# Splitting float32 operands on another engine, and finishing attention blocks in smaller steps

## The chip, the cores and the metric

The kernel runs on one core of a Trainium2 chip. The metric is the device time of one execution in microseconds. The engines are TensorE (PE in the profile; PEld is its loading of weights), VectorE (DVE), ScalarE (ACT), GpSimd (POOL) and SyncE (SP), which issues most of the DMAs.

## What is computed

For x of 2048 x 512 in float32:

```python
qkv = x @ wqkv                                   # 32 heads of 16
scores = einsum("hqd,hkd->hqk", q, k) * 16**-0.5
scores = where((q - k >= 0) & (q - k < 256), scores, -1e9)
a = (softmax(scores) @ v) @ wo
b = (silu(x @ w_gate) * (x @ w_up)) @ w_down     # width 1792
g = sigmoid((x * gate_w).sum(-1))
out = g * a + (1 - g) * b
```

## The kernel before, in words

**Two halves.** Each float32 operand of a large product is split into a high half (rounded to the type that TensorE takes at full speed) and a low half, `src - high` (`split`, lines 68 to 73). A product is three matmuls: high by high, high by low, low by high. ScalarE casts the high half; the low half is one subtraction of two operands in SBUF, on GpSimd or VectorE as the caller says.

**Start (lines 401 to 512).** The first weights of Q and K (groups 0 and 1) come in two pieces each; `split_wq` splits a piece. x comes in four chunks of 512 columns, each of four k blocks; `split_x(c)` splits a chunk, its low halves on VectorE. V's weights (four k blocks, `wvh`, `wvl`) are split in the loop of lines 484 and 485: high on ScalarE, low on GpSimd for even k and on VectorE for odd k. TensorE then computes the first projections (`proj`), the first four blocks of V (`vproj`, each 12 matmuls that go through k in order: high by high, high by low, low by high), and further projections. `put_v` is ScalarE's copy of a V block out of PSUM. After this come the row maxima of group 0.

**The main loop (lines 697 to 726)** has 129 turns `t`. Heads are in eight groups of four; a turn handles one block of 128 queries or keys of one group, and has four *steps*, one a head. Four turns make a *quad*, numbered here from 0 (`d` in the code), with parts 0 to 3; step (p, h) is step h of part p. In each step the program order is:

- `stage1` of the next group: a score matmul (line 302) into one of two PSUM banks `ps1`, and VectorE's masked row maximum (line 304, followed by a short instruction that reads out the accumulator). The score matmul of a step can start only when the maximum two steps before is done. Only quads 0 to 27 have this stage.
- `stage2` of this group: a score matmul the other way round (line 344), ScalarE's exp (line 346), and in every second step GpSimd's `affine_select` (lines 348, 351), which zeroes what the window leaves out.
- six matmuls of a projection or of the FFN (line 252).
- what was put into `AT` for this step: splits, FFN products, loads.
- one step of `finish`, where the list of line 714 says so.

**Finishing a block of values.** In step (0,1) of each quad from 1 on, `av` multiplies the probabilities of the quad before by V (line 368), into two PSUM tiles. `finish` (lines 375 to 399) then runs in steps, as a Python generator that is advanced by `run(FIN, 1)`: ScalarE copies one tile (line 383), VectorE adds the other (385, and 387 in some quads), transposes (389), takes the reciprocal of the softmax sums and multiplies by it (393, 394; 128 x 256 elements), and transposes back (397); GpSimd issues the DMA to DRAM (398). Each `yield` ends a step. Before the change the steps are: copy in (0,1), addition in (0,2), transposition in (1,1), reciprocal with multiplication in (1,3), transposition and DMA in (2,1).

**What else stands in `AT`.** `halve_next` splits the next FFN or projection weights: ScalarE casts, GpSimd subtracts (`wl`, line 73, 128 x 512). Lines 546 to 559 put it at step 1 of part 0, or at step 0 of part 2 or of part 3. `group_half` splits the projections of a later group (`xlo`, line 73, also GpSimd) in steps (0,0) to (1,1) of some quads. VectorE's products of the FFN (lines 571 and 583) stand in (3,0), (3,1), (3,3) and (0,0), a sum (585) in (1,0). In quads 26 to 31 the token gate's products (638) stand in (1,2) and (2,2), and from quad 28 on the splits of w_down (`early`, lines 641 to 663, with casts at line 654) in part 0.

Each engine takes its instructions in program order; the order above is written out by hand.

Of the kernel before, what the change touches and what calls it, by code (L numbers as in the profile page):

```python
# [12 lines left out]
ALU = mybir.AluOpType  # L13
# [3 lines left out]
P = 128  # L17
S, D, H, DH, W, F = 2048, 512, 32, 16, 256, 1792
NK = D // P
NB = S // P  # L20
CH = 512
# [15 lines left out]
def gated_mix(ctx, tc, xT, xn, wqk, wv, wo, wgu, wd, gw, outT):  # L37
# [4 lines left out]
    nc = tc.nc  # L42
# [25 lines left out]
    def split(hi, lo, src, hi_eng, lo_eng):  # L68
        if hi_eng is nc.scalar:
            nc.scalar.copy(hi, src)  # L70
        else:
            hi_eng.tensor_copy(hi, src)
        lo_eng.tensor_tensor(out=lo, in0=src, in1=hi.bitcast(F32), op=ALU.subtract)

    def fetch(src, raw=None):

        raw = ring.tile([P, D], F32, name="raw", bufs=1) if raw is None else raw
        nc.sync.dma_start(raw, src)
        return raw

    def by_k(t):
        return t.rearrange("p (k n) -> p k n", k=NK)
# [11 lines left out]
    def run(gen, n=None):  # L94

        while n is None or n > 0:
            if next(gen, run) is run:
                break
            n = n and n - 1
# [73 lines left out]
    def prefetch():  # L173
        if WKEYS:
            PEND.append(weights(WKEYS[0], lo_eng=nc.vector if WKEYS.pop(0) == ('f', NF - 1, 0) else nc.gpsimd))
# [25 lines left out]
    with ExitStack() as A:  # L201
# [14 lines left out]
        def kept():  # L216
            return sm.tile([P, CH], F32, name="ev", bufs=EV)
# [10 lines left out]
        def whole(pool, name, todo, done):  # L228

            ps = pool.tile([P, CH], F32, name=name)  # L230
            for n, (w, x) in enumerate(todo):
                nc.tensor.matmul(ps, w, x, start=n == 0, stop=n == len(todo) - 1)  # L232
                if n < len(todo) - 1:
                    yield
            done(ps)
            yield
# [91 lines left out]
        def load_v(n):  # L328

            VG[n] = sm.tile([P, 4, VW], F32, name="vg", bufs=4)  # L330
            nc.sync.dma_start(VG[n], vd[n // 4, :, n % 4 * 4:n % 4 * 4 + 4])
# [43 lines left out]
        def finish(g, c):  # L375


            first, second = AV[g, c]
            if not AB:
                AB.extend(osb.tile([P, CH], F32, name=f"o{n}") for n in range(2))  # L380
            both, ot = AB[::-1] if c % 2 else AB
            lo = 0 if c else 64
            nc.scalar.copy(both[:, lo:], second[:, lo:])
            yield
            nc.vector.tensor_tensor(out=both[:, lo:], in0=first[:, lo:], in1=both[:, lo:], op=ALU.add)  # L385
            if lo:
                nc.vector.tensor_copy(both[:, :lo], first[:, :lo])
            yield
            nc.vector.transpose(ot, both)
            yield  # L390
            v = ot.rearrange("p (s e) -> p s e", e=32)
            rc = osb.tile([P, CH // 32], F32, name="rc")
            nc.vector.reciprocal(rc, v[:, :, DH])
            nc.vector.tensor_tensor(out=v[:, :, :DH], in0=v[:, :, :DH],
                                    in1=rc[:, :, None].to_broadcast([P, CH // 32, DH]), op=ALU.mult)
            yield
            nc.vector.transpose(both, ot)
            nc.gpsimd.dma_start(od[g, :, c * CH:(c + 1) * CH], both)
            yield
# [3 lines left out]
        wvh = vpool.tile([P, NK, D], F32R, name="wvh")  # L403
        wvl = vpool.tile([P, NK, D], F32R, name="wvl")
# [8 lines left out]
        def split_wq(g, n, lo_eng):  # L413
            if n == 0:
                WT["p", g] = [ring.tile([P, D], F32R, name=w) for w in ("wh", "wl")]
            hi, lo = (w[:, QUARTERS[n]] for w in WT["p", g])
            split(hi, lo, WQ[g][:, QUARTERS[n]], nc.scalar, lo_eng)
            if n == 1:
                WT["p", g] = [by_k(w) for w in WT["p", g]]
# [3 lines left out]
        def fill_rows(tiles, value, hf, eng):  # L423
            for t in tiles:
                eng.memset(halves_of(t)[hf].bitcast(F32), value)
# [3 lines left out]
        def fill_v(t):  # L429
            nc.gpsimd.memset(t, 0.0)  # L430
            for i in range(2):
                nc.gpsimd.memset(t[:, :, i, :68].rearrange("p g (j e) -> p g j e", e=17)[:, :, :, DH], 1.0)
# [3 lines left out]
        def v_products(b):  # L436
            c, o = divmod(b * P, CH)
            return [(xt[c][:, k, o:o + P], wt[:, k]) for k in range(NK)
                    for xt, wt in ((xhi, wvh), (xhi, wvl), (xlo, wvh))]

        def put_v(b, ps):
            t = vs[b // 2 % 2]
            nc.scalar.copy(t[:, :, b % 2, :68].rearrange("p g (j e) -> p g j e", e=17)[:, :, :, :DH],
                           ps.rearrange("p (g j e) -> p g j e", j=4, e=DH))
            if b % 2:
                nc.gpsimd.dma_start(vd[:, :, b - 1:b + 1].rearrange("g p b e -> p g (b e)"),
                                    t.rearrange("p g b e -> p g (b e)"))

        def vproj(b):
            return whole(pp, "pb", v_products(b), lambda ps: put_v(b, ps))  # L450
# [11 lines left out]
        def split_x(c, ks=range(NK)):  # L462
            for k in ks:
                split(xhi[c][:, k], xlo[c][:, k], xraw[2 * c + k // 2][k % 2], nc.scalar, nc.vector)

        for c in range(NCH):
# [7 lines left out]
            if c == 0:  # L474
                wvraw = [fetch(wv[:, k], kept()) for k in range(NK)]
        split_wq(0, 0, nc.gpsimd)
        split_x(0, range(1))
        split_wq(1, 0, nc.vector)
        split_wq(0, 1, nc.gpsimd)
        fill_rows(KT[0], 1.0, 0, nc.gpsimd)  # L480
        split_x(0, range(1, 2))
        split_wq(1, 1, nc.vector)
        split_x(0, range(2, NK))
        for k in range(NK):
            split(wvh[:, k], wvl[:, k], wvraw[k], nc.scalar, nc.vector if k % 2 else nc.gpsimd)
        prefetch()
        both = [proj(g, 0, pp, "pa") for g in range(2)]
        for k in range(NK):
            for gen in both:
                run(gen, 3)  # L490
        split_x(1)
        fill_v(vs[1])
        fill_rows(QT[0], 0.0, 1, nc.gpsimd)
        fill_rows(KT[0], 1.0, 1, nc.gpsimd)
        for b in range(2):
            run(vproj(b))
        split_x(2)
        for b in range(2, 4):
            run(vproj(b))
# [43 lines left out]
        def later(t, hd, *fs):  # L543
            AT.setdefault((t, hd), []).extend(fs)
# [65 lines left out]
        def unit(t):  # L610

            def both(n, name):
                key, hf = TURNS[t // 2 + n]
                done = (group_half(t, key[1], hf) if key[0] == "p" else (gate_half, up_half)[key[2]](t, key[1], hf))
                two = []

                def turn(m):
                    if not two:
                        two.extend(lanes(pp, name, [products(key, 2 * hf + m) for m in range(2)], done))
                    yield from two[m]  # L620
                return turn(0), turn(1)
            (a0, a1), (b0, b1) = (both(n, name) for n, name in enumerate(("pa", "pb")))
            return [a0, b0, a1, b1]
# [55 lines left out]
        for b in range(NB):  # L679
            t, hd = blocks[b]  # L680
            later(t, hd, lambda b=b: gate_block(b))
            if b > 1:
                t, hd = blocks[b - 2]
# [13 lines left out]
        FIN = iter(())  # L697
        for t in range(G * NB + 1):
            g, i = divmod(t, NB)
            d, part = divmod(t, NSLOT)  # L700
            if part == 0:
                turns = unit(t) if t < G * NB else [iter(())] * NSLOT
            s1 = stage1(g + 1, i) if t < g7 else iter(())
            s2 = stage2(g, i) if t < G * NB else iter(())
            for hd in range(4):
                run(s1, 1)
                if t < g7:
                    run(s2, 1)
                elif hd % 2 == 0:
                    run(s2, 2)  # L710
                run(turns[part], 3)
                for f in AT.pop((t, hd), ()):
                    f()
                if (part, hd) in ((0, 2), (1, 1), (1, 3), (2, 1)):
                    run(FIN, 1)
                if hd == 1 and part == 0:
                    if t:
                        ag, c = divmod(d - 1, NCH)
                        av(ag, c)
                        FIN = finish(ag, c)  # L720
                        run(FIN, 1)
            if i in (7, 15) and g + 1 < G:
                later(t + 1, 2, lambda g=g, i=i: put_max(g + 1, i // 8))
            if t >= 10 and t % 4 == 2 and t + 6 < G * NB:
                load_v((t + 6) // 4)
# [6 lines left out]
    with ExitStack() as B:  # L732
# [7 lines left out]
        def column():  # L740
            return hp.tile([P, CH], F32, name="sg", bufs=4)
# [300 lines left out]
        for n, e in enumerate(ITEMS[:end]):  # L1042
# [13 lines left out]
            p, k, pr = e  # L1056
# [6 lines left out]
        two, t, part, rest = bank(4, 1), *(column() for _ in range(3))  # L1063
# [46 lines left out]
```

## Time and profile before

| | us |
|---|---|
| median of 3 runs | 803.44 (803.0 to 803.46) |
| the profiled execution, its time | 803.47 |
| its span, first to last instruction | 801.8 |
| TensorE busy | 795.2 (99%) |
| VectorE busy | 627.3 (78%) |
| ScalarE busy | 432.4 (54%) |
| GpSimd busy | 346.2 (43%) |

The times of the profile are measured from the start of the span. An engine's busy time is the union of its instructions. Ends of matmuls are modelled, so their starts are the better measure. "Idle before" in brackets is how long the engine stood idle before an instruction, with what ended the wait.

### The profile page before, as it was taken

Reading aid. Unit: us, or ns where it says so; the run is one execution under the profiler, and the core shown is the slowest. Engines: PE = TensorE matmul, PEld = TensorE weight load, DVE = VectorE, ACT = ScalarE, POOL = GpSimd, SP = SyncE. Lnnn points to the kernel's source line nnn. Section 1 sums busy time; section 2 is a strip of 40 time slices with the busy share of each in tenths; the row PEclk is TensorE's granted clock in tenths of the full one; section 3 lists DMA queues with packets and bytes.
Section 4 is the critical chain, followed back from the end, with each engine's and each line's share of the span. In section 5 each row is a group of like instructions: output and inputs, shape, how many; then the busy total and the mean of one; then the engine's idle time right before and its main releaser. Section 6 shows DMA issues by size and latency. Waiting matters only on the chain.

```text
span 801.8 us, 21443 instructions
## 1 busy us (share of the span) xinstructions
PE 795.2 (99%) x8247; PEld 697.1 (87%) x8247; DVE 627.3 (78%) x1686; ACT 432.4 (54%) x883; POOL 346.2 (43%) x647
## 2 busy tenths in 40 slices
PE   8999999999999999999999999999999999999998
PEld 7888999989889989889998988888988888888886
DVE  6397687878887787878777878888675478899896
ACT  6412656666566566555666656555643235554642
POOL 7821546564546556544656454546740111000212
PEclk9999999999999999999999999999999999999999
DMA  8675414434252453351444516435627898718435
GB/s 298 171 200 164 141 57 135 119 114 137 71 164 78 117 167 94 113 163 54 134 119 130 152 46 200 134 99 181 195 100 240 283 342 300 290 56 275 93 54 104
DMA packets 62107, 121.88 MB, mean 152 GB/s; under 512 B 10868, under 2 KB 19828, under 8 KB 61748
## 3 DMA queue, kind: packets, MB, share of 16 engines
q1 hardware_dynamic: 54900, 99.27, 40.1%
q0 software_dynamic: 7104, 21.24, 9.0%
q8 instruction: 65, 1.06, 0.6%
q14 instruction: 38, 0.31, 0.1%
HBM read 55.97 MB, written 39.34 MB: 119 GB/s over the span
## 4 chain that ended last, share of the span: by engine, by line
PE 96%; DVE 2%; DMA 1%; SPq 0%; POOL 0%; issue 0%; ACT 0%
PE pa L252 24%; PE pb L252 24%; PE ps L302 7%; PE ps L344 5%; PE ps L368 5%; PE ps L89 4%; PE ps L90 4%; PE ps L88 4%; PE pb L368 4%; PE pb L232 2%; PE pb L89 2%; PE pa L89 2%; PE pa L90 2%; PE pb L90 2%; PE pa L88 2%; PE pb L88 2%
## 5 line engine op out<-in xcount | busy, mean ns | idle before, releaser
L304 DVE CUSTOM_DVE_ANT_0 ps<-ps,mask 128x384 f32<-128x384 f32 (+2 forms) x512 | 268.4, 540 | 99.4 <-PE ps L344 52.3
L346 ACT ACTIVATE pt<-ps 128x384 f32<-128x384 f32 (+2 forms) x512 | 238.0, 474 | 127.8 <-PE ps L344 68.0
L348 POOL TENSOR_SCALAR_AFFINE_SELECT pt<-pt 128x256 f32<-128x256 f32 x256 | 110.2, 431 | 198.6 <-ACT pt L346 196.8
L344 PE MATMUL ps<-q,k 64*128 64x384 f32 (+2 forms) x512 | 162.3, 334 | 0.0
L302 PE MATMUL ps<-k,q 63*128 63x384 f32 (+2 forms) x512 | 159.8, 332 | 0.5 <-DVE mx L304 0.5
L252 PE MATMUL pb<-xhi,wh 64*128 64x512 f32 x512 | 116.9, 395 | 0.0
L252 PE MATMUL pb<-xlo,wh 64*128 64x512 f32 x512 | 115.6, 391 | 0.0
L252 PE MATMUL pb<-xhi,wl 64*128 64x512 f32 x512 | 115.6, 391 | 0.0
L252 PE MATMUL pa<-xhi,wh 64*128 64x512 f32 x512 | 115.3, 393 | 0.0
L252 PE MATMUL pa<-xlo,wh 64*128 64x512 f32 x512 | 114.2, 391 | 0.0
L252 PE MATMUL pa<-xhi,wl 64*128 64x512 f32 x512 | 114.2, 391 | 0.0
L302 PEld LDWEIGHTS ps<-k,q 63*128 63x128 f32 x512 | 88.7, 185 | 14.1 <-DVE mx L304 3.7
L351 POOL TENSOR_SCALAR_AFFINE_SELECT pt<-pt 128x256 f32<-128x256 f32 x224 | 98.6, 440 | 0.0
L344 PEld LDWEIGHTS ps<-q,k 64*128 64x128 f32 x512 | 91.1, 184 | 4.9 <-ACT pt L346 0.2
L304 DVE DVE_READ_ACCUMULATOR2_ANT mx<- 128x1 f32 x512 | 71.3, 139 | 0.0
L368 PE MATMUL ps<-pt,vg 64*32 64x320 f32 (+4 forms) x1408 | 70.6, 344 | 0.0
L368 PE MATMUL pb<-pt,vg 64*32 64x256 f32 (+3 forms) x1360 | 69.9, 349 | 0.0
L252 PEld LDWEIGHTS pb<-xhi,wh 64*128 64x128 f32 x512 | 62.8, 185 | 4.1 <-DVE o L385 0.3
L252 PEld LDWEIGHTS pb<-xhi,wl 64*128 64x128 f32 x512 | 62.4, 184 | 3.5
L252 PEld LDWEIGHTS pa<-xhi,wl 64*128 64x128 f32 x512 | 61.1, 185 | 3.9
L252 PEld LDWEIGHTS pb<-xlo,wh 64*128 64x128 f32 x512 | 62.5, 185 | 0.2
L252 PEld LDWEIGHTS pa<-xhi,wh 64*128 64x128 f32 x512 | 60.5, 186 | 1.8
(305 smaller groups left out, 1604.5 us busy)
## 6 DMA issues: line engine op xcount, KB each, us to landing
kept_h<-ev SPq DMA_DIRECT2D x52, 256.0 KB
od<-o POOLq DMA_DIRECT2D x32, 256.0 KB, 3.7
raw<-wgu SPq DMA_DIRECT2D x28, 256.0 KB
q<-xhi SPq DMA_DIRECT2D x56, 128.0 KB
k<-xhi SPq DMA_DIRECT2D x56, 128.0 KB
outT<-sg POOLq DMA_DIRECT2D x28, 256.0 KB, 4.4
vd<-vs POOLq DMA_DIRECT2D x8, 672.0 KB, 4.8
vg<-vd SPq DMA_DIRECT2D x32, 168.0 KB
```

The source lines that it names most:

```text
L88: nc.tensor.matmul(ps, lh, rh, start=start and i == 0, stop=False, skip_group_check=skip)
L89: nc.tensor.matmul(ps, lh, rl, start=False, stop=False, skip_group_check=skip)
L90: nc.tensor.matmul(ps, ll, rh, start=False, stop=stop and i == n - 1, skip_group_check=skip)
L232: nc.tensor.matmul(ps, w, x, start=n == 0, stop=n == len(todo) - 1)
L252: mm = nc.tensor.matmul(ps[me], w[r], x[r], start=not second and i == 0, stop=bool(second) and i == n - 1)
L302: nc.tensor.matmul(ps[:, :n], QT[g % 2][pr][r, q0:q0 + P], KT[g % 2][pr][r, k0:k0 + n], start=True, stop=True)
L304: mx = nc.vector.tensor_tensor_reduce(out=ps[:, :n], in0=ps[:, :n], in1=mask[:, 3 * P - n:], scale=1.0, scalar=NEG, op0=ALU.add, op1=ALU.m ...
L344: nc.tensor.matmul(ps[:, :n], KT[g % 2][pr][r, k0:k0 + P], QT[g % 2][pr][r, k0:k0 + n], start=True, stop=True)
L346: BEHIND.append(nc.scalar.activation(pt[:, j, :n], ps[:, :n], AF.Exp, scale=SCALE))
L348: nc.gpsimd.affine_select(out=pt[:, :, :P], in_=pt[:, :, :P], pattern=[[0, 2], [1, P]], compare_op=ALU.is_ge, fill=0.0, base=0, channel_mu ...
L351: nc.gpsimd.affine_select(out=pt[:, :, 2 * P:], in_=pt[:, :, 2 * P:], pattern=[[0, 2], [-1, P]], compare_op=ALU.is_ge, fill=0.0, base=-1, ...
L368: nc.tensor.matmul(AV[g, c][h][32 * j:32 * j + 32, q0 - c * CH:q1 - c * CH], VG[4 * g + kb // 4][o, kb % 4, 17 * j:17 * j + 32], PT[g, kb, ...
```

## The change

Three edits. First, the low half of the second piece of group 0's weights, and the low halves of V's weights for even k, go from GpSimd to VectorE; the splits of the second x chunk are issued after V's first and second block, two k blocks each. Second, in `finish` the reciprocal is a step of its own, and the multiplication becomes two instructions of 128 x 128 elements, a step each. Third, the list of steps in which `finish` is advanced becomes (0,2), (1,1), (1,3), (2,0), (2,1), (2,2), and the advance comes ahead of `AT` in its step. So the reciprocal stands in (1,3), the halves of the multiplication in (2,0) and (2,1), the transposition with the DMA in (2,2).

```diff
             nc.vector.reciprocal(rc, v[:, :, DH])
-            nc.vector.tensor_tensor(out=v[:, :, :DH], in0=v[:, :, :DH],
-                                    in1=rc[:, :, None].to_broadcast([P, CH // 32, DH]), op=ALU.mult)
             yield
+            for s in (slice(0, CH // 64), slice(CH // 64, CH // 32)):
+                nc.vector.tensor_tensor(out=v[:, s, :DH], in0=v[:, s, :DH],
+                                        in1=rc[:, s, None].to_broadcast([P, CH // 64, DH]), op=ALU.mult)
+                yield
             nc.vector.transpose(both, ot)
...
-        split_wq(0, 1, nc.gpsimd)
+        split_wq(0, 1, nc.vector)
...
-            split(wvh[:, k], wvl[:, k], wvraw[k], nc.scalar, nc.vector if k % 2 else nc.gpsimd)
+            split(wvh[:, k], wvl[:, k], wvraw[k], nc.scalar, nc.vector)
...
-        split_x(1)
         fill_v(vs[1])
...
         for b in range(2):
             run(vproj(b))
+            split_x(1, range(2 * b, 2 * b + 2))
         split_x(2)
...
+                if (part, hd) in ((0, 2), (1, 1), (1, 3), (2, 0), (2, 1), (2, 2)):
+                    run(FIN, 1)
                 for f in AT.pop((t, hd), ()):
                     f()
-                if (part, hd) in ((0, 2), (1, 1), (1, 3), (2, 1)):
-                    run(FIN, 1)
```

## Rows read from the trace of the kernel before

**Rows 1.** The page, busy time and share of the span of each engine.
```profile
PE 795.2 (99%) x8247; PEld 697.1 (87%) x8247; DVE 627.3 (78%) x1686; ACT 432.4 (54%) x883; POOL 346.2 (43%) x647
```

**Rows 2.** Waits of the weight loads: who <- whom: us in total, times, longest.
```profile
PEld ps L302 <- DVE mx L304: 3.7, 11, 0.7
...
PEld pb L232 <- POOL wvl L73: 1.3, 2, 0.9
```

**Rows 3.** Timelines by engine (start, us, engine, line, [idle before]): quad 7; last, quad 15.
```profile
201.07 1.27 POOL L73 TENSOR_TENSOR xlo<-ev,xhi 128x512 fp32r<-128x512 f32 x1
...
201.48 1.15 DVE L394 TENSOR_TENSOR o<-o,rc 128x256 f32<-128x256 f32 x1
202.55 0.55 DVE L304 CUSTOM_DVE_ANT_0 ps<-ps,mask 128x384 f32<-128x384 f32 x1
...
201.71 0.18 PEld L302 LDWEIGHTS ps<-k,q 63*128 63x128 f32 x1
203.22 0.18 PEld L302 LDWEIGHTS ps<-k,q 63*128 63x128 f32 x1 [0.67 <-DVE mx L304]
...
332.38 1.16 DVE L394 TENSOR_TENSOR o<-o,rc 128x256 f32<-128x256 f32 x1
```

**Rows 4.** Line 394: count, ns least/median/most, first and last start.
```profile
L394 DVE TENSOR_TENSOR o<-o,rc x32: 424/474/1155, 103.3 to 602.0; 128x256 f32<-128x256 f32 x32
```

**Rows 5.** Timelines by engine, steps (2,0) to (3,1) of quad 5.
```profile
169.56 1.29 POOL L73 TENSOR_TENSOR wl<-raw,wh 128x512 fp32r<-128x512 f32 x1 [0.38 <-ACT wh L70]
...
169.34 0.57 DVE L304 CUSTOM_DVE_ANT_0 ps<-ps,mask 128x384 f32<-128x384 f32 x1
...
169.83 0.70 DVE L397 STREAM_TRANSPOSE o<-o 128x512 f32<-128x512 f32 x1
...
170.47 0.18 PEld L302 LDWEIGHTS ps<-k,q 63*128 63x128 f32 x1
171.32 0.18 PEld L302 LDWEIGHTS ps<-k,q 63*128 63x128 f32 x1
172.21 0.18 PEld L302 LDWEIGHTS ps<-k,q 63*128 63x128 f32 x1
```

**Rows 6.** Timeline of the start of the kernel.
```profile
5.26 0.28 DVE L73 TENSOR_TENSOR wl<-ev,wh 128x128 fp32r<-128x128 f32 x1
...
6.82 1.01 POOL L73 TENSOR_TENSOR wl<-raw,wh 128x384 fp32r<-128x384 f32 x1 [2.03 <-ACT wh L70]
...
10.09 0.69 DVE L73 TENSOR_TENSOR xlo<-q,xhi 128x512 fp32r<-128x512 f32 x1 [0.64 <-ACT xhi L70]
...
11.02 2.57 ACT L70 CAST wvh<-ev 128x512 fp32r<-128x512 f32 x4 [0.96 <-DMA ev<-wv]
...
11.71 3.00 POOL L73 TENSOR_TENSOR wvl<-ev,wvh 128x512 fp32r<-128x512 f32 x2 [2.11 <-ACT wvh L70]
...
12.01 0.39 PE L232 MATMUL pa<-xhi,wl 128*128 128x512 f32 x1
...
12.23 0.39 PE L232 MATMUL pb<-wvh,xhi 128*128 128x512 f32 x1
...
13.05 0.50 PE L232 MATMUL pb<-wvl,xhi 128*128 128x512 f32 x1 [0.43 <-POOL wvl L73]
```

**Rows 7.** Tile wl alone, busy by stretch, first and last of six (step (2,1)).
```profile
121.00:122.40 1.40, 0.88 (x4) 0.26 (x2) 0.00 (x0) 1.29 (x1) 1.00 0.02 6
...
431.20:432.70 1.50, 0.80 (x4) 0.25 (x4) 0.00 (x0) 1.29 (x1) 1.00 0.00 0
```

The columns are the length, then PE, PEld, DVE and POOL with their counts, the clock, the DMA share and GB/s. The other four stretches begin at 169.5, 251.9, 300.4 and 382.7.

**Rows 8.** Timeline of VectorE, step (2,2) of quad 26.
```profile
515.13 0.68 DVE L638 SCALAR_TENSOR_TENSOR xhi<-xlo,xhi 128x512 f32<-128x512 f32 x1
```

**Rows 9.** Timelines of VectorE and ScalarE, step (0,2) of quad 28.
```profile
539.17 1.85 DVE L654 CAST q<-ev 128x512 fp32r<-128x512 f32 x2
...
541.27 0.65 DVE L385 TENSOR_TENSOR o<-pb,o 128x512 f32<-128x512 f32 x1
...
540.00 0.59 ACT L383 COPY o<-ps 128x512 f32<-128x512 f32 x1 [1.10 <-PE pb L368]
```

## The prediction, made before the changed kernel was run

> **What bounds the kernel now.** I read the page first. TensorE is busy for 99% of the span [rows 1]. So the time changes only where TensorE starts to wait or stops waiting, and a microsecond saved on VectorE or GpSimd is worth nothing by itself. Next I read the list of waits for the engine that loads weights [rows 2]: there the reader sees the two kinds of wait that the change can touch, the score matmul of line 302 waiting for the row maxima of line 304, and the first V matmuls waiting for low halves that GpSimd makes. Last I read the timeline around those places. Sums are made against the profiled execution: 803.47 us, of which 801.8 is its span and 1.67 lies around it; it stands 0.03 over the median of the runs.
>
> **First mechanism: a port that one engine holds.** In quad 7 the multiplication of line 394 starts at 201.48, while GpSimd's subtraction runs from 201.07 to 202.34. It ends at 202.63, so 0.29 after GpSimd [rows 3], and it takes 1.15 where the 32 have a median of 0.47 and a least of 0.42 [rows 4]. It does not run slower, it stands still. The reciprocal just before it was not held (it was over by 201.48, with GpSimd at work since 201.07), nor is a transposition beside such a subtraction (0.70, [rows 5]). The Trainium skill (SBUF — State Buffer, Who interferes with whom) has the rule: a VectorE instruction with two SBUF inputs and a GpSimd instruction that reads SBUF exclude each other, and the one that starts first keeps the port to its end. The trace agrees (1.15 against 0.42); were the bandwidth shared instead, a block would stay within the slack of the two score banks and the term of the six quads below would be near 0, which is the second case's time. This rule speaks for one half of the change and against the other.
>
> **Start: low halves by VectorE.** The second V matmul waits until 13.05 for a low half that GpSimd begins at 11.71; the matmul before it started at 12.23, and these follow each other by 0.22 (12.01 to 12.23), so it came 0.6 late. Of two such waits, 1.3 together, the list puts 0.9 on this one and so 0.4 on a second [rows 2]; the load of weights runs ahead of its matmul, so of the two I count 0.6 and 0.3. ScalarE's four high halves take 2.57 from 11.02, so the first is there at 11.66; VectorE, with nothing of GpSimd beside it, needs 0.69 for such a subtraction (the 512-wide one at 10.09), so the low half is there at 12.4 and the matmul can go at 12.45. The next come every 0.69, as fast as three matmuls of 0.22 use them up. Gain: 0.6 + 0.3 = **0.9**. The first weights' low half (GpSimd, 6.82 to 7.83, [rows 6]) becomes earlier by about 0.4 on VectorE, but that only makes TensorE wait longer for V: 0. Bounds of the stage: 0.5 (the later low halves come late by a little each) to 1.0. Moving the second x chunk's splits behind V's first two blocks costs nothing: their first user is the projection behind four V blocks, 48 matmuls or 10.6 us later, and VectorE has eight subtractions of 0.69, 5.5 us, to do in that time; without this cover a late chunk would cost up to those 5.5. GpSimd's memory fills start earlier and have no reader that waits.
>
> **The finish in smaller steps, ordinary quads.** A full multiplication of 0.42 becomes two of 0.28 (VectorE's two-input instruction of 128 elements at the start took that, [rows 6]); since an instruction starts some 0.07 before the last one ends, VectorE has about 0.1 more work a quad. The score steps last about 0.87 (the weights of line 302 at 170.47, 171.32 and 172.21 are 0.85 and 0.89 apart, [rows 5]), one maximum holds VectorE for 0.5 (169.34 to 169.83), so 0.37 is free in each step: a half of 0.21 net fits, a transposition of 0.63 net is made good by the free step behind it. Cost 0 with that cover; without it 0.1 in each of the 27 quads that have both, 2.7, is the bound. Waits fall on nobody new: the reciprocal's reader now comes one step later. The output DMA on GpSimd's queue goes out one step later, and GpSimd's selects of steps (2,3) and (3,1) queue behind it; their reader is the value sum of the next quad, so 0.
>
> **Two quads gain.** In quad 7 the weights of line 302 are loaded at 201.71 and then at 203.22, 1.51 apart instead of 0.87 [rows 3]: 0.64 lost. Quad 15 has the same pattern (1.16 at 332.38, [rows 3]). With the reciprocal alone in step (1,3), the maximum of (2,0) no longer stands behind the blocked multiplication; the first half then starts near 202.0, is held until 202.34 and ends by 202.48, some 0.1 after the maximum of (2,1) could start, and the two banks hide that. Gain 2 x 0.6 = **1.2**. In the other quads GpSimd's work lengthens the multiplication by less: its median is 0.05 over its least [rows 4], 1.3 for 25 quads; taking that out of a step in which a bank is waited for is worth 0 to 1.3, and I take **0.4**, near the small end, because the waits of line 302 are 3.7 in all, of which 1.3 is already counted [rows 2].
>
> **Six quads lose.** Here the steps were moved past work of GpSimd. Weights' low halves that are due at step (2,0) run on GpSimd in quads 2, 5, 10, 13, 18 and 21, 1.29 in the first and the last [rows 7]. Until now only a transposition ran beside them, and it is not blocked (0.70, [rows 5]). Now the second half stands in its place. In quad 5: GpSimd holds the port from 169.56 to 170.85; the second half comes at 169.83, 0.27 too late, and ends 0.14 after GpSimd (the tail of 0.29, less the 0.14 that 128 elements save). So the maximum of (2,2) starts at 170.92 instead of 170.46. The transposition, now in step (2,2), starts 0.48 later (169.34 to 169.83 shows that step), takes 0.63 net, and the maximum of (2,3) starts at 172.03. Its bank is free 0.62 + 0.05 later (202.55 to 203.22, [rows 3]), at 172.70. The score matmul of step (3,1) wanted it at 172.21: 0.49 lost, of which 0.27 already at (3,0). The other quads, by the same arithmetic, give up to 0.65, as steps alternate in length. I take 0.55: 6 x 0.55 = **3.3** lost (2.9 to 3.9). The lead of GpSimd rests on ScalarE's cast, which follows TensorE and not VectorE, so the change does not move it.
>
> **Two more quads lose a little.** In quads 26 and 27 the token gate's product of line 638, 0.68, already stands in step (2,2) [rows 8], and now the transposition comes into the same step; VectorE is without a gap there, so the second multiplication instruction's 0.1 is paid in each: **0.2** (0.1 to 0.7).
>
> **Order inside a step.** The finish step now comes ahead of what is due in that step. In quad 28 that matters: two casts of 1.85 (blocked by GpSimd) stand in front of the addition of line 385, which frees a bank and starts only at 541.27, 0.68 after ScalarE's copy was there at 540.59 [rows 9]. Now it goes first: gain **0.2** (0 to 0.45).
>
> Sum: -0.9 - 1.2 - 0.4 + 3.3 + 0.2 - 0.2 = +0.8; 803.47 + 0.8 gives 804.3.
>
> **Rivals.** *The six blocks don't happen or are absorbed.* Either the second half comes before GpSimd's subtraction, or the score banks hide the wait. For it: the margin is 0.27 of 1.29. Against it: the same order of start led to the full block in quad 7. The sum without 3.3 is -2.5: 801.0.
> *The blocks cost their whole length.* Place: the same six, steps (2,1) to (3,1). The half (1.16 from 169.83) and the transposition behind it delay the maxima with no slack left, because the two products of line 571 at (3,0) and (3,1) keep VectorE from catching up. Price 1.0 each, 6.0 instead of 3.3: 807.0. From 0.68 a block on, the whole is slower by over 0.2%. For it: both banks are already at their limit in quad 7. Against it: in quad 7 a block of 0.86 cost 0.64.
>
> **How the numbers follow.** 0.2% (1.6 us) is about what a measurement of this kernel can tell from no change: under 801.8, or over 805.0. My case has 0.70; its own range is 803.0 to 805.6, by the bounds above, and it gives 0.48 to no change and 0.22 to slower. The first rival has 0.20 (0.17 faster, 0.03 the same), the second 0.10, all slower. Together: faster 0.17, same 0.51, slower 0.32. The range 800.8 to 805.8 takes in my case and the first rival, and leaves out the second.
>
> **What would show it.** Right: the second V matmul starts by about 12.5; 64 multiplications of about 0.28, of which six last over 1.0, all in step (2,1) of the quads named; the weights of line 302 wait more than the 3.7 of now, with the waits at (3,0) and (3,1) of those six; quads 7 and 15 lose their 0.67. Wrong: no multiplication above 0.6 (then the first rival), or six waits of 1.0 (the second). If the V matmuls still wait beyond 12.5, the start term is wrong; if new waits of line 302 turn up in the other quads, the cover was not there.

## The result and the profile after

The changed kernel takes 806.29 us (median of 11 executions, 804.37 to 808.55) against 803.55 for the kernel before on the same chips (802.54 to 804.38): 1.0033 of it, with an interval of 1.0026 to 1.0041. It is slower, and outside the forecast range.

There are two losses. The profiled execution took 804.64, 1.17 over that of before. It is one of four executions whose mean granted clock is 0.999 or 1.0 (804.37 to 805.29); the other seven have 0.995 to 0.998 and take 806.01 to 808.55. What the four show is told first; the rest is a matter of the clock (experiment 9).

The page again shows a busy TensorE, and VectorE and GpSimd have traded work:

```profile
PE 794.2 (99%) x8247; PEld 686.8 (86%) x8247; DVE 630.9 (79%) x1721; ACT 432.7 (54%) x883; POOL 335.4 (42%) x644
```

To see where the time went, I measure each quad from its first weight load of line 344 to that of the next.

| place | before | after | difference |
|---|---|---|---|
| start, up to quad 0 | 79.70 | 78.78 | -0.92 |
| quads 7, 15 | 16.90 each | 16.40 each | -1.00 |
| quad 23 | 16.74 | 16.40 | -0.34 |
| quads 6, 14, 22 | 16.60, 16.62, 16.62 | 16.43 each | -0.55 |
| quads 2, 5, 10, 13, 21 | 81.61 in all | 83.30 | +1.69 |
| quad 18 | 16.63 | 16.54 | -0.09 |
| quads 26, 27 | 33.53 | 33.41 | -0.12 |
| quad 28 | 15.47 | 17.66 | **+2.19** |
| quad 29 | 14.80 | 14.93 | +0.13 |
| the rest, differences up to 0.05 a quad, and the tail | | | +0.18 |

The start went as forecast. In the timeline of the changed kernel the second V matmul (wvl) follows the first after 0.23, where it came 0.82 after it, at 13.05, before [rows 6]:

```profile
10.75 2.64 DVE L73 TENSOR_TENSOR wvl<-ev,wvh 128x512 fp32r<-128x512 f32 x4 [0.53 <-ACT wvh L70]
...
12.39 0.39 PE L232 MATMUL pb<-wvh,xhi 128*128 128x512 f32 x1
12.62 0.39 PE L232 MATMUL pb<-wvl,xhi 128*128 128x512 f32 x1
```

In quad 7 (timeline of the changed kernel) the weights of line 302 are loaded 0.86 and 0.81 apart, where one gap was 1.51 [rows 3]. The half of the multiplication is still lengthened, but only to 0.50:

```profile
201.63 0.50 DVE L396 TENSOR_TENSOR o<-o,rc 128x128 f32<-128x128 f32 x1
...
201.37 0.18 PEld L302 LDWEIGHTS ps<-k,q 63*128 63x128 f32 x1
...
202.23 0.18 PEld L302 LDWEIGHTS ps<-k,q 63*128 63x128 f32 x1
...
203.04 0.18 PEld L302 LDWEIGHTS ps<-k,q 63*128 63x128 f32 x1
```

The held halves came too. Line 396 with its least, median and longest duration in ns, and rows of quad 5 in the changed kernel, from the second half in step (2,1) to the load of step (3,2):

```profile
L396 DVE TENSOR_TENSOR o<-o,rc x64: 282/289/1262, 102.7 to 603.5; 128x128 f32<-128x128 f32 x64
```

```profile
168.99 1.30 POOL L73 TENSOR_TENSOR wl<-raw,wh 128x512 fp32r<-128x512 f32 x1 [0.56 <-ACT wh L70]
...
169.25 1.19 DVE L396 TENSOR_TENSOR o<-o,rc 128x128 f32<-128x128 f32 x1
170.36 0.55 DVE L304 CUSTOM_DVE_ANT_0 ps<-ps,mask 128x384 f32<-128x384 f32 x1
...
169.90 0.19 PEld L302 LDWEIGHTS ps<-k,q 63*128 63x128 f32 x1
...
171.02 0.18 PEld L302 LDWEIGHTS ps<-k,q 63*128 63x128 f32 x1 [0.29 <-DVE mx L304]
...
172.10 0.18 PEld L302 LDWEIGHTS ps<-k,q 63*128 63x128 f32 x1 [0.36 <-DVE mx L304]
...
172.84 0.18 PEld L302 LDWEIGHTS ps<-k,q 63*128 63x128 f32 x1
```

The half comes 0.26 behind GpSimd's subtraction and ends 0.15 after it, and two loads of line 302 wait, 0.65 together. The next load follows after only 0.74, so part of that is made good: quad 5 is 0.33 longer, not 0.65. In quad 18 the order of the two starts is the other way round, and nothing is held:

```profile
381.94 0.29 DVE L396 TENSOR_TENSOR o<-o,rc 128x128 f32<-128x128 f32 x1
...
382.05 1.34 POOL L73 TENSOR_TENSOR wl<-raw,wh 128x512 fp32r<-128x512 f32 x1 [0.93 <-ACT wh L70]
```

**Quad 28** is the loss that the forecast doesn't have. `put_max` (lines 311 to 321), which is due in step (0,2) of this quad by line 723, turns the row maxima (lines 315, 316), stores them to DRAM (`md`, line 318) and reads them back into the q tiles (line 320), both on SyncE's queue. Behind these two in the queue stand the loads of weights, of xn and of w_down, and then two writes of FFN products (`kept_h`, line 588 before, 590 after). Timelines of VectorE, SyncE's queue (SPq) and ScalarE around it, before:

```profile
535.57 0.27 PEld L344 LDWEIGHTS ps<-q,k 64*128 64x128 f32 x2
...
541.13 0.21 DVE L316 STREAM_TRANSPOSE mtt<-mt 128x32 f32<-128x32 f32 x1
...
541.38 0.58 SPq L318 DMA_DIRECT2D md<-mtt  x1
543.37 0.99 SPq L320 DMA_DIRECT2D q<-md  x2
...
545.80 0.90 SPq L588 DMA_DIRECT2D kept_h<-ev  x2
...
549.87 0.60 ACT L568 ACTIVATE ev<-pa 128x512 f32<-128x512 f32 x1 [0.16 <-DMA kept_h<-ev]
```

and after:

```profile
534.25 0.27 PEld L344 LDWEIGHTS ps<-q,k 64*128 64x128 f32 x2
...
539.30 0.69 DVE L385 TENSOR_TENSOR o<-pb,o 128x512 f32<-128x512 f32 x1 [0.34 <-ACT o L383]
539.91 0.96 DVE L656 CAST q<-ev 128x512 fp32r<-128x512 f32 x2
...
541.20 0.21 DVE L316 STREAM_TRANSPOSE mtt<-mt 128x32 f32<-128x32 f32 x1
...
549.25 0.69 DVE L640 SCALAR_TENSOR_TENSOR xhi<-xlo,xhi 128x512 f32<-128x512 f32 x1 [2.79 <-DMA xlo<-xn]
...
541.44 0.58 SPq L318 DMA_DIRECT2D md<-mtt  x1
544.03 0.99 SPq L320 DMA_DIRECT2D q<-md  x2
...
546.48 0.90 SPq L590 DMA_DIRECT2D kept_h<-ev  x2
...
550.88 0.60 ACT L570 ACTIVATE ev<-pa 128x512 f32<-128x512 f32 x1 [2.87 <-DMA kept_h<-ev]
...
551.91 0.83 PE L344 MATMUL ps<-q,k 64*128 64x384 f32 x2 [2.03 <-ACT pt L346]
```

Read it against the start of the quad. The addition of line 385 now heads the step and waits for ScalarE's copy, which ends at 5.02 in both kernels. (The wait shows as 0.34 here because VectorE's sums before it are held beside GpSimd in this profile; where they are not, in the second profile of the same kernel under experiment 9, it is 1.37, and the addition starts at the same 5.05.) The casts, which began 3.60 after the start (539.17 in [rows 9], less 535.57), begin at 5.66, and `put_max` is behind them. The store goes out at 7.19 instead of 5.81, the read back at 9.78 instead of 7.80, the writes at 12.23 instead of 10.23. ScalarE's tanh (line 570) takes the buffer that such a write empties. It already waited 0.16 for it before; now it waits 2.87, the exps queue behind it, and TensorE stands still for 2.03.

### The profile page after: what moved, and what is told of

It is laid out like the page before. It is cut to its first block, busy times and chain, and to the rows that moved or that the text cites. A ratio compares the mean times of both kernels' runs of the same rounds, so it can differ in the third digit from the quotient of the medians.

```text
span 802.9 us, 21471 instructions
## 1 busy us (share of the span) xinstructions
PE 794.2 (99%) x8247; PEld 686.8 (86%) x8247; DVE 630.9 (79%) x1721; ACT 432.7 (54%) x883; POOL 335.4 (42%) x644
## 4 chain that ended last, share of the span: by engine, by line
PE 96%; DVE 1%; DMA 1%; ACT 0%; SPq 0%; issue 0%
PE pa L252 24%; PE pb L252 24%; PE ps L302 7%; PE ps L368 5%; PE ps L344 5%; PE ps L90 4%; PE ps L89 4%; PE ps L88 4%; PE pb L368 4%; PE pb L232 2%; PE pa L232 2%; PE pa L90 2%; PE pb L90 2%; PE pb L88 2%; PE pa L89 2%; PE pb L89 2%
## 5 line engine op out<-in xcount | busy, mean ns | idle before, releaser
L348 POOL TENSOR_SCALAR_AFFINE_SELECT pt<-pt 128x256 f32<-128x256 f32 x256 | 106.9, 418 | 192.7 <-ACT pt L346 192.0
L252 PE MATMUL pb<-xhi,wh 64*128 64x512 f32 x512 | 111.3, 395 | 0.0
L252 PE MATMUL pa<-xlo,wh 64*128 64x512 f32 x512 | 110.4, 391 | 0.0
L252 PE MATMUL pa<-xhi,wl 64*128 64x512 f32 x512 | 110.1, 391 | 0.0
L252 PE MATMUL pb<-xlo,wh 64*128 64x512 f32 x512 | 109.7, 391 | 0.0
L252 PE MATMUL pb<-xhi,wl 64*128 64x512 f32 x512 | 109.7, 392 | 0.0
L351 POOL TENSOR_SCALAR_AFFINE_SELECT pt<-pt 128x256 f32<-128x256 f32 x224 | 95.5, 427 | 0.0
L252 PEld LDWEIGHTS pb<-xhi,wl 64*128 64x128 f32 x512 | 56.8, 185 | 5.4
L252 PEld LDWEIGHTS pb<-xhi,wh 64*128 64x128 f32 x512 | 56.8, 186 | 4.9
L252 PEld LDWEIGHTS pa<-xhi,wh 64*128 64x128 f32 x512 | 56.7, 186 | 3.1
L252 PEld LDWEIGHTS pa<-xlo,wh 64*128 64x128 f32 x512 | 57.8, 186 | 0.2
```

The lines of the kernel that those rows point to most:

```text
L252: mm = nc.tensor.matmul(ps[me], w[r], x[r], start=not second and i == 0, stop=bool(second) and i == n - 1)
L348: nc.gpsimd.affine_select(out=pt[:, :, :P], in_=pt[:, :, :P], pattern=[[0, 2], [1, P]], compare_op=ALU.is_ge, fill=0.0, base=0, channel_mu ...
L351: nc.gpsimd.affine_select(out=pt[:, :, 2 * P:], in_=pt[:, :, 2 * P:], pattern=[[0, 2], [-1, P]], compare_op=ALU.is_ge, fill=0.0, base=-1, ...
```

## The experiments

Medians are beside those of the kernel before from the same chips. The theory to test: the new order inside a step delays SyncE's queue in quad 28, the held halves are a smaller second loss, and the lowered clock follows TensorE's stand-still. Its rivals: the finer steps themselves cost it (more instructions, held halves), or the lowered clock comes from elsewhere.

**1. The finish behind `AT` again**, all else as changed.

```diff
-                if (part, hd) in ((0, 2), (1, 1), (1, 3), (2, 0), (2, 1), (2, 2)):
-                    run(FIN, 1)
                 for f in AT.pop((t, hd), ()):
                     f()
+                if (part, hd) in ((0, 2), (1, 1), (1, 3), (2, 0), (2, 1), (2, 2)):
+                    run(FIN, 1)
```

> The changed kernel with one part undone: the finish step comes behind what is due in its step again. Queue theory (in quad 28 the finish step ahead of the row-maximum store makes that store late, the DMA queue of SyncE late behind it, a buffer of line 570 late, and TensorE waits 2.4 us, after which its clock is lower in some executions): quad 28 takes about 15.4 us instead of 17.7, the time is 802.2 (801.8 to 802.7), and every execution has a clock of 0.999 or more. Block theory (the held multiplications are the loss and its spread): the time stays near 806, and clocks below 0.999 turn up again.

Measured: 803.14 against 803.67, ratio 0.9993 (0.9984 to 1.0002); quad 28 is 15.72, every execution has a clock of 0.999 or 1.0. So without the new order neither the loss of quad 28 nor the lowered clock is there. The median is higher than expected: the five held halves stay, and quads 6, 14 and 22 fall back to the old length (quad 6: 16.63), so the order also had a gain that I had put down to the shorter multiplication.

**2. The order alone**, in the kernel before, with its four old steps.

```diff
+                if (part, hd) in ((0, 2), (1, 1), (1, 3), (2, 1)):
+                    run(FIN, 1)
                 for f in AT.pop((t, hd), ()):
                     f()
-                if (part, hd) in ((0, 2), (1, 1), (1, 3), (2, 1)):
-                    run(FIN, 1)
```

> The kernel before with one part of the change alone: the finish step ahead of what is due in its step, the old steps and the old engines. Queue theory: quad 28 stalls, by 1 to 2.5 us, and executions with a clock below 0.999 turn up; time 804.5 to 807. Block theory: no change beyond 0.3 us, 803.5.

Measured: 804.09 against 803.67, ratio 1.0005 (0.9996 to 1.0014). Quad 28 is 16.86 instead of 15.47, and quad 6 is 16.45: the order alone gives the gain, and 1.39 of the 2.19 lost in quad 28. The time lies under the 804.5 to 807 expected, and none of the 11 executions has a clock under 0.999, which misses that part of the expectation too. The stand-still of TensorE is 1.2 here:

```profile
PE ps L344 <- ACT pt L346: 1.2, 1, 1.2
```

**3. The start alone**, in the kernel before.

```diff
-        split_wq(0, 1, nc.gpsimd)
+        split_wq(0, 1, nc.vector)
...
-            split(wvh[:, k], wvl[:, k], wvraw[k], nc.scalar, nc.vector if k % 2 else nc.gpsimd)
+            split(wvh[:, k], wvl[:, k], wvraw[k], nc.scalar, nc.vector)
...
-        split_x(1)
...
             run(vproj(b))
+            split_x(1, range(2 * b, 2 * b + 2))
```

> The kernel before with the first edit alone (low halves by VectorE, the second x chunk's splits later). Both theories: the second V matmul goes at about 12.5, the first turn of the main loop starts 0.9 us earlier, and the time is 802.6 (802.3 to 803.0), with clocks of 1.0. Against it: if what is earlier at the start only meets a queue further on, 803.5.

Measured: 802.49 against 803.67, ratio 0.9988 (0.9979 to 0.9996). Quad 0 begins at 78.76, 0.94 earlier. Quad 23 is 16.41 here too, so its 0.34 in the table doesn't come from the finish. It is 16.43 in experiment 5 too, which has none of the three edits; what it comes from I don't know.

**4. `put_max` one step earlier**, in the changed kernel: the order stays, only the queue gets its store sooner.

```diff
-                later(t + 1, 2, lambda g=g, i=i: put_max(g + 1, i // 8))
+                later(t + 1, 1, lambda g=g, i=i: put_max(g + 1, i // 8))
```

> The changed kernel with one thing moved: the store of the row maxima is due one step earlier, (0,1) instead of (0,2), so that it is ahead of the addition and the casts of that step. Queue theory: the stall of quad 28 goes as in the first run, 802.2 (801.6 to 802.7), clocks 0.999 or more. Rival: if the casts or the token gate's product are what is late, quad 28 stays above 17 us and the time near 806.

Measured: 802.15 against 803.67, ratio 0.9982 (0.9973 to 0.9991), clocks 0.999 or 1.0. Its timelines show the store 5.14 after the start of the quad and a tanh that doesn't wait:

```profile
534.13 0.27 PEld L344 LDWEIGHTS ps<-q,k 64*128 64x128 f32 x2
...
539.27 0.57 SPq L318 DMA_DIRECT2D md<-mtt  x1
...
543.76 0.90 SPq L590 DMA_DIRECT2D kept_h<-ev  x2
...
548.02 0.60 ACT L570 ACTIVATE ev<-pa 128x512 f32<-128x512 f32 x1
```

The five held halves are all still there, so they alone don't make the change slower than the kernel before.

**5. `put_max` one step later in the kernel before**, to bring the stall into a kernel that has nothing of the change.

```diff
-                later(t + 1, 2, lambda g=g, i=i: put_max(g + 1, i // 8))
+                later(t + 1, 3, lambda g=g, i=i: put_max(g + 1, i // 8))
```

> The kernel before with the store of the row maxima due one step later, (0,3), and nothing else. Queue theory: its order on VectorE is 2.4 us later in quad 28, which takes 18 to 19 us instead of 15.5; time 806 to 808 and clocks below 0.999 in some executions, with no part of the change in the kernel. Rival (it is the finish step's new place that matters, not the store): 803.5 to 804.0.

Measured: 809.44 against 803.46, ratio 1.0078 (1.0064 to 1.0092); quad 28 is 19.58. All five executions have a clock of 0.995 to 0.998. The direction is right, the size was too small. Quad 16, which also has such a store, takes 16.95 instead of 16.10. In quad 28 TensorE stands still for 3.9, and then runs at half clock (stretch, length, busy time of PE, PEld, DVE, ACT and POOL, granted clock, DMA share, GB/s):

```profile
552.00:555.00 3.00, 0.00 (x0) 0.00 (x0) 1.41 (x4) 0.74 (x2) 0.00 (x0) 1.00 1.00 360
555.00:557.00 2.00, 1.71 (x7) 1.61 (x9) 1.77 (x3) 1.49 (x4) 0.81 (x3) 0.50 0.85 301
```

**6. The two writes of quad 28 on GpSimd's queue**, in the changed kernel, to see whether they alone are what is waited for.

```diff
-                    later(t + 5, 2, lambda m=m: nc.sync.dma_start(kept_h[f, 2 * hf + m], hs[m]))
+                    later(t + 5, 2, lambda m=m: (nc.gpsimd if g7 <= t + 5 < g7 + 4 else nc.sync).dma_start(kept_h[f, 2 * hf + m], hs[m]))
```

> The changed kernel with one thing moved: the two writes of line 590 in quad 28 are issued on GpSimd's queue instead of SyncE's, so that they don't stand behind the row-maximum store; that store stays late. Queue theory with the buffer: line 570 gets its buffer early, quad 28 takes 15.2 to 16.0 us instead of 17.4 to 17.7, time 802.2 to 803, no clock below 0.999. Rival (the other transfers in SyncE's queue, the loads of x for the token gate, are what TensorE waits for): quad 28 stays above 17, time 805 to 806.

Measured: 806.07 against 803.85, ratio 1.0030 (1.0018 to 1.0041). Neither theory had it whole: quad 28 is short, as the first said, and the loads of xn are what is waited for, as the second said, but in quad 29. The tanh no longer waits, and quad 28 is 15.09. But VectorE's token-gate product now waits 4.10 for its load of xn from SyncE's queue (2.79 in the changed kernel), and TensorE waits for VectorE in quad 29:

```profile
548.25 0.62 ACT L570 ACTIVATE ev<-pa 128x512 f32<-128x512 f32 x1
...
551.08 0.69 DVE L640 SCALAR_TENSOR_TENSOR xhi<-xlo,xhi 128x512 f32<-128x512 f32 x1 [4.10 <-DMA xlo<-xn]
...
552.43 1.39 PE L252 MATMUL pa<-xhi,wh 64*128 64x512 f32 x2 [2.01 <-DVE ev L573]
```

So two paths stand behind these transfers, and taking one away leaves the other. The load of xn goes out at the same place in both kernels, 11.34 and 11.30 after the start of the quad, but the product that waits for it starts at 16.46 instead of 15.00. The order of the transfers fits this: the two writes, at 12.23 behind the load in the changed kernel, now go out at 9.94, ahead of it,

```profile
544.56 1.10 POOL L590 DMA_DIRECT2D kept_h<-ev  x2
```

and from 11 to 13 after the start 0.49 of the 0.57 MB that are moved are GpSimd's queue's. That this is the cause was not tried by itself. Four of the seven executions have a clock of 0.995 to 0.998, among them the profiled one (808.19): behind its stand-still of 2.01 the granted clock is 0.50 for 6.8, and quad 29 takes 20.60.

**7. The whole multiplication as one instruction at (2,0)**, the reciprocal alone at (1,3), the transposition at (2,1): first with `put_max` one step earlier, then where the change has it. Both go from the changed kernel; the second is without the last two lines.

```diff
-            for s in (slice(0, CH // 64), slice(CH // 64, CH // 32)):
-                nc.vector.tensor_tensor(out=v[:, s, :DH], in0=v[:, s, :DH],
-                                        in1=rc[:, s, None].to_broadcast([P, CH // 64, DH]), op=ALU.mult)
-                yield
+            nc.vector.tensor_tensor(out=v[:, :, :DH], in0=v[:, :, :DH],
+                                    in1=rc[:, :, None].to_broadcast([P, CH // 32, DH]), op=ALU.mult)
+            yield
...
-                if (part, hd) in ((0, 2), (1, 1), (1, 3), (2, 0), (2, 1), (2, 2)):
+                if (part, hd) in ((0, 2), (1, 1), (1, 3), (2, 0), (2, 1)):
...
-                later(t + 1, 2, lambda g=g, i=i: put_max(g + 1, i // 8))
+                later(t + 1, 1, lambda g=g, i=i: put_max(g + 1, i // 8))
```

> The changed kernel with the store of the row maxima one step earlier, and with the multiplication whole again, in step (2,0), the transposition in (2,1). Both theories: no multiplication is held in the quads 2, 5, 10, 13 and 21, which take 16.4, 16.1, 16.4, 16.1 and 16.1 us; the quads 7 and 15 keep their gain of 0.5; time 800.2 (799.8 to 800.8), clocks 0.999 or more. Against the held port: if the halves themselves cost the time, and not the port, those quads stay at 16.9 and 16.5.

> The changed kernel with the multiplication whole in step (2,0) and the transposition in (2,1), the store left where the change has it. Queue theory with the clock: quad 28 still takes 17.4 to 17.8 us, the best executions are near 802.6, and others with clocks of 0.998 or less lie 1.5 to 4 us above. If the low clocks come from the many small waits of the held halves, they are gone here, and all executions lie near 802.6.

Measured: 799.50 against 803.46, ratio 0.9949 (0.9936 to 0.9961), with the store earlier, a little under the 799.8 to 800.8 expected; this version is faster than both kernels. With the store as changed 801.47, ratio 0.9976 (0.9966 to 0.9985); quad 28 is 16.93 and TensorE stands still for 1.3, under the 17.4 to 17.8 expected, and no clock is under 0.999. In the first of them the longest multiplication takes 0.65 (1.15 in the kernel before), and of the waits of line 302 0.8 is left, of 5.4 in the changed kernel:

```profile
L395 DVE TENSOR_TENSOR o<-o,rc x32: 416/422/647, 103.0 to 598.2; 128x256 f32<-128x256 f32 x32
```

```profile
PEld ps L302 <- DVE mx L304: 0.8, 4, 0.3
```

**8. Both halves in one step, (2,0)**, from experiment 4: still two instructions, but none at (2,1), where GpSimd's subtraction runs.

```diff
             for s in (slice(0, CH // 64), slice(CH // 64, CH // 32)):
                 nc.vector.tensor_tensor(out=v[:, s, :DH], in0=v[:, s, :DH],
                                         in1=rc[:, s, None].to_broadcast([P, CH // 64, DH]), op=ALU.mult)
-                yield
+            yield
...
-                if (part, hd) in ((0, 2), (1, 1), (1, 3), (2, 0), (2, 1), (2, 2)):
+                if (part, hd) in ((0, 2), (1, 1), (1, 3), (2, 0), (2, 1)):
```

> The changed kernel with the store one step earlier and both halves of the multiplication in step (2,0), the transposition in (2,1): two instructions as in the change, but both ahead of GpSimd's subtraction. Held port: the quads 2, 5, 10, 13 and 21 take 16.55, 16.1, 16.55, 16.1 and 16.1 us as with the whole product, and the time is 799.5 to 800.0. If two instructions instead of one were the cost, they take 16.9 and 16.5 and the time is near 802.

Measured: 799.97 against 803.85, ratio 0.9954 (0.9941 to 0.9966). Quads 2, 5, 10, 13 and 21 are 16.55, 16.14, 16.53, 16.11 and 16.11, and the longest half takes 0.52:

```profile
L396 DVE TENSOR_TENSOR o<-o,rc x64: 282/286/523, 102.5 to 598.7; 128x128 f32<-128x128 f32 x64
```

So it is the place of the second half beside GpSimd's subtraction that costs, not its being an instruction of its own. The transposition, which this edit moves too, from (2,2) to (2,1), is not what costs in these quads: quad 18 of the changed kernel has it in (2,2) and its half not held, and takes 16.54, against 16.53 here.

**9. The clock.** First the changed kernel once more, unedited, for a profile of an execution with a lowered clock.

> The changed kernel once more, for the spread of its times, beside the others on the same chip. Clock theory (TensorE's wait of 2.4 us in quad 28 is followed in most executions by a stretch at the lower clock): the median is 805.5 to 806.5, executions fall into a group near 804.5 with clocks of 0.999 and 1.0 and others 1.5 to 4 us above it with 0.998 or less; a profile of such an execution shows the granted clock below 1 behind 549 us. Rival (another chip or day): all executions near 804.5, clocks of 0.999 and 1.0.

Measured: 805.40 against 803.46, ratio 1.0027 (1.0018 to 1.0037); five of ten executions have 0.997 or 0.998 (805.76 to 806.99), the others 1.0 (804.66 to 805.03). The profiled one is of the first kind. TensorE stands still for 1.78 before 551.40, and then the windows show a granted clock near 0.5 (0.50 in each microsecond from 553 to 555), so 1.2 GHz of 2.4, for 3.4 in all; quad 29 takes 16.52 where it took 14.93 with the clock at 1.00:

```profile
549.00:552.00 3.00, 1.22 (x8) 0.58 (x6) 1.93 (x5) 1.48 (x4) 0.20 (x1) 1.00 1.04 371
552.00:554.00 2.00, 2.00 (x12) 1.95 (x11) 1.62 (x4) 0.75 (x2) 1.33 (x4) 0.56 0.77 282
554.00:556.00 2.00, 2.00 (x35) 1.08 (x40) 1.18 (x3) 0.00 (x0) 0.00 (x0) 0.59 0.00 0
```

Then the stand-still was filled: nine matmuls more behind step (3,3) of quad 28, into a bank that nothing reads, with the late queue as it is.

```diff
+                if t == g7 + 3 and hd == 3:
+                    idle = ps1.tile([P, CH], F32, name="ps1")
+                    for _ in range(9):
+                        nc.tensor.matmul(idle, xhi[0][:, 0, :P], xhi[0][:, 0], start=True, stop=True)
```

> The changed kernel with nine more matmuls of 128 x 512 behind quad 28's last step, about 2.0 us of TensorE work on data that is there, into a bank that nothing reads; the result doesn't depend on them. They lie in the stretch in which TensorE stood still for about 2.0 us; the late queue stays as it is, so the path should not grow by more than 0.3. Theory that the lowered clock of some executions comes from TensorE's standing still: the mean granted clock is 0.999 or 1.0 in every execution, no two-to-three-us half clock, the median 804.4 to 805.2. Rival, that the clock falls for something else in these stages (the transfers' burst, the mix of work): low clocks in about half of the executions as before, median 805.4 to 806.3.

Measured: 805.01 against 803.51, ratio 1.0019 (1.0010 to 1.0028); all 11 executions have 0.999 or 1.0. The wait on the queue is still there (the tanh waits 2.6, quad 28 is 17.82), but TensorE has work in it, and in its timeline and windows the clock stays:

```profile
550.50 2.33 PE L721 MATMUL ps<-xhi 128*128 128x512 f32 x9
552.77 0.44 PE L344 MATMUL ps<-q,k 64*128 64x384 f32 x2
```

```profile
549.00:552.00 3.00, 3.00 (x20) 2.39 (x19) 1.39 (x4) 0.72 (x2) 0.54 (x2) 1.00 0.99 367
552.00:554.00 2.00, 2.00 (x16) 1.44 (x16) 1.79 (x3) 1.40 (x4) 0.77 (x2) 1.00 1.03 376
```

The transfers in these two stretches (367 and 376 GB/s) are about as many as where the clock fell (371 and 282), or more, so they are not what lowers it.

## Why the prediction was wrong

**The step that failed is "Order inside a step".** It said that the finish, going first in step (0,2) of quad 28, gains 0.2; the quad lost 2.19. It looked at the addition alone, and at the 0.68 by which it came after ScalarE's copy [rows 9]. It didn't ask what is queued behind an instruction that now waits: the casts, which need nothing of that copy, and `put_max` behind them, whose result goes through SyncE's queue. The runs give the price of a late queue. Times are from the start of quad 28:

| kernel | store of the maxima | read back | writes `kept_h` | TensorE stands still | quad 28 |
|---|---|---|---|---|---|
| experiment 7, store earlier | 5.13 | 7.13 | 9.58 | 0 | 15.08 |
| experiment 4 | 5.14 | 7.13 | 9.63 | 0 | 15.11 |
| before | 5.81 | 7.80 | 10.23 | 0 | 15.47 |
| experiment 1 | 5.80 | 7.80 | 10.25 | 0 | 15.72 |
| experiment 2 | 7.19 | 9.19 | 11.63 | 1.2 | 16.86 |
| experiment 7, store as changed | 7.19 | 9.18 | 11.62 | 1.3 | 16.93 |
| changed | 7.19 | 9.78 | 12.23 | 2.0 | 17.66 |
| experiment 5 | 9.06 | 11.05 | 13.49 | 3.9 | 19.58 |

From 10.23 on, a queue that is later by 1.40, 2.00 or 3.26 makes the quad longer by 1.39, 2.19 or 4.11 (why the last is more than its delay is open). The kernel before had no slack left here: its tanh waited 0.16 for such a write, a row that I could have read. Of the changed kernel's 2.00, 1.38 is the order. The other 0.6 is the store itself, which takes 2.59 to 2.62 until the read back instead of 1.99 to 2.00, in all four profiles that have the changed kernel's finish, order and place of the store (the changed kernel twice, experiments 6 and 9) and in no other. The listing of the DMA packets shows what differs. Between the store and the read back it has, in the changed kernel (541.44 to 544.03),

```profile
q1 hardware_dynamic: 132, 0.02, 4.2%
q14 instruction: 1, 0.01, 1.1%
```

and in experiment 7 with the store as changed (539.14 to 541.13)

```profile
q1 hardware_dynamic: 132, 0.02, 5.3%
```

(queue and kind, packets, MB, share of the DMA engines). In the four profiles one packet of 8192 bytes of the kind that the listing calls instruction begins 1.12 or 1.13 after the store, among the store's own packets, the last of which then ends at 1.90 to 1.99; in the other nine none lies there, and the last ends at 1.57 to 1.59. So the 0.6 goes with that packet; that the packet makes it was not tried.

**The second failure is the clock, which the forecast doesn't have at all.** It is what takes the median out of the range. The seven executions with a lowered clock have a median of 806.86, 2.3 over the middle of the other four (804.53). Seven of eleven decide the median. That a stand-still is what lowers it rests on experiment 9: the filled wait takes lowered clocks from 12 of 21 executions to none of 11. That the other four lie near the forecast of 804.3 is luck: quad 28 cost 2.4 more than its term, and the six quads 1.7 less than theirs.

**The start** was right: -0.92 for the -0.9 forecast, -0.94 alone in experiment 3. A pair of profiles tells this only to some tenths: quad 0 begins at 78.47 to 79.45 in the ten profiles with the first edit, and at 79.57 to 80.36 in the three without. The second V matmul comes at 12.62, not by 12.5, but the one before it is also 0.16 later than it was, and the wait between them is gone.

**Two quads** were right in place and near in size: -1.00 for -1.2.

**The other quads' -0.4** came to -0.55 in quads 6, 14 and 22, for another reason. Experiment 2 has it with the old multiplication (16.43 to 16.45), and so has experiment 5 with the old order but with `put_max` out of step (0,2) (16.43). So it is the addition no longer standing behind `put_max`, and not the shorter multiplication, that gives it.

**The six quads** were right in mechanism and too large in size. The rule that the forecast took from the Trainium skill (SBUF — State Buffer, Who interferes with whom), that the instruction that starts first keeps the port, agrees with the trace: the five halves that start 0.18 to 0.26 behind GpSimd take 1.19 to 1.26, and the one that starts 0.11 ahead takes 0.29. Five quads lose 0.32 to 0.38 against before, 0.33 to 0.43 against experiment 8 (1.86 in all), where I took 0.55 each. Up to step (3,1) the arithmetic was near: the two gaps between loads of quad 5 are 0.27 and 0.19 longer, 0.46 in all for the 0.49 forecast. But the term stopped there, with the largest delay. The next gap is 0.74 instead of 0.85 and gives 0.11 back, and the 0.65 reckoned for other quads is not there (at most 0.38 against before). In the sixth, quad 18, a premise failed: GpSimd's subtraction began 0.23 ahead of what VectorE had in that place before (382.79 against 383.02), and now begins 0.11 behind the half, so the change did move its lead.

**Quads 26 and 27** lost nothing in all (-0.12 for +0.2), but the cost forecast is there: with the transposition back in (2,1), experiment 8 has 16.75 and 16.30, where experiment 4 has 16.97 and 16.43. Something else in the changed kernel pays for it, which was not tried alone.

**The rivals** were both about the six quads. The second, at 807.0, lies near the measured median, but its mechanism is not there: a held half cost 0.34, not 1.0. Without the stall in quad 28 the change is a gain, 802.15 in experiment 4.

## What to carry to other kernels

When an instruction that waits is moved ahead of others in its engine's program order, list everything behind it up to the next DMA that some queue issues in order, and follow that queue to its last reader: here one addition held up two casts, a small store, all that stood behind it on its queue and, 10 us later, TensorE. Where the trace of before shows even a short wait at the end of such a chain (0.16 here), there is no slack, and each microsecond of delay was paid in full. An instruction with two SBUF inputs is best put into a step in which GpSimd doesn't read SBUF: taking the second half out of GpSimd's way was worth 1.8 in the five quads (experiment 4 against 8).

## What the runs showed of the hardware that was not expected

The granted clock fell behind some stand-stills of TensorE, in a part of the executions of one and the same kernel. Counted over all executions, those under 0.999 are none of 20 where the profile shows a stand-still of 1.2 or 1.3 in these quads (experiments 2 and 7, the latter with the store as changed), 16 of 28 where it shows 1.8 to 2.0 (the changed kernel, twice, and experiment 6), and all 5 where it shows 3.9 (experiment 5); none of 43 in the kernels that have no such wait (experiments 1, 3, 4, 8, and 7 with the store earlier). Three falls were profiled: the clock is at 0.50 for 3.4 in experiments 5 and 9 and for 6.8 in experiment 6, and in experiment 9 quad 29 is 1.59 longer than in the same kernel at full clock. Why the same wait is followed by a fall in one execution and not in the next was not tried.
